# Transposes of the next group's tokens as steps among the current group's slices

## The chip, the cores and the metric

The kernel runs on one core of one Trainium2 chip. The metric is the time of one execution in microseconds on the device (us). TensorE is called PE here (its weight loads PEld), VectorE DVE, ScalarE ACT, GpSimd POOL, and SyncE, which issues all transfers of this kernel, SP.

## The reference

Three layers follow each other: causal attention blended with a linear memory, then two gated feed-forward layers over all tokens (4 batches of 576 tokens, 8 heads of 64, 512 channels, 1536 hidden channels).

```python
scores = where(causal, -1e9, q @ k.T / sqrt(D));  a = softmax(scores)
local = a @ v
q_p = phi(q)                                    # elu + 1
mem = (q_p @ M_prev) / (q_p @ z_prev + 1e-6)
x = g * mem + (1 - g) * local                   # g = sigmoid(beta), by head
x = x / sqrt(mean(x * x) + 1e-6) * rms_g
x = (silu(x @ w_gate) * (x @ w_val)) @ w_out    # layer 0
x = (sigmoid(x @ w_gate2) * (x @ w_val2)) @ w_out2   # layer 1
```

## The kernel before, in words

The tokens are worked in five groups. Group -1 holds the first 128 tokens of each of the four batches (512 tokens); its attention is done before everything else (`att_first`). Groups 0 to 3 are the other 448 tokens of batches 0 to 3. The outer loop `for g in range(-1, B)` runs the two feed-forward layers of group g, and among their work it does the attention of group g+1. Group 3 has no attention beside it.

A layer has 12 slices of 128 hidden channels. `hidden` makes a slice's gate `pg` and value `pv` (12 matmuls each, L502; two PSUM buffers of the pool `psm` for both), ACT and DVE make the product `t` from them (L517, L519 and L520 in layer 0, L517 and L522 in layer 1) and split it into two parts `h` (L524 on ACT, L525 on DVE), and `out_share` adds the slice's share into four PSUM tiles `po` (L536, L539). After the last slice `evacuate` empties the four `po`: into the next layer's input `x` (L545 on ACT, L546 on DVE), or to the output (L557, L559). In group -1 the weights come from 64-bit floats (L453, L456) and are split in two parts (L427, L428), in group 0 they are split once more and the parts stored, later groups load the parts. PE works most products three times, high by high, high by low and low by high.

Attention comes as a list of 30 steps for a group (`att_steps`): one that loads the values `v` into the tile `x` and scales them (`att_v`: the loads L125 and L126, then the maximum `am` over the tile on DVE, L128), for each head `att_qk` and `att_scores` (matmuls L186 into tiles of the PSUM pool `psa`, which has two buffers of tag `pa`; DVE and ACT work L264 to L306, L177 to L180), `att_av` (L313 to L324), for each pair of heads `att_mem` (L357 to L386), and at the end `att_norm`. `x` has one buffer: the values of group g+2 can be loaded only when the tokens of group g+1 have been read out of it.

After 23 of the 24 slices of a group, and after all its steps, `run_xT` turned the next group's tokens: four times `att_xT`, which normalises 128 tokens (`xn`, L403 on DVE), transposes them with four matmuls (`pxt`, L408, a tile of the same two `pa` buffers), and copies them out in two parts (L412 on ACT, L413 on DVE) into `xt`, the input of the next group's layer 0.

Steps are taken by the count of slices whose share has been added, `done`:

```python
while used < len(steps) and used < len(steps) * done // total:
    steps[used]()
    used += 1
```

with `total` = 21. This gives the order in which the program is written. The build then schedules the instructions by a timeline of its own (`schedule_with_timeline_sim=True`), so each engine's final order can differ from it; it is fixed before the run, and each engine works through its own list in order.

Of the kernel before, what the change touches and what calls it, by code (L numbers as in the profile page):

```python
# [33 lines left out]
def attn_moe_moe_kernel(ctx, tc, qT, kT, v, mz, beta, w8, rms_g, outT):  # L34
# [11 lines left out]
    NF = w8.shape[1]  # L46
# [66 lines left out]
    for i in range(2):  # L113
        t = const.tile([128, S], F32R, name=f"q2_{i}")
# [6 lines left out]
    st = {}  # L121
# [266 lines left out]
    def att_norm(g, t0, t1):  # L388
        x = st[g]["x"]
        ss = ap_.tile([128, 4], F32, tag="ss", bufs=2, name="ss")  # L390
        for t in range(t0, t1):
            junk = z["s", t, 0] if g < 0 else ap_.tile([128, DM], F32, tag="xn", bufs=2, name="junk")
            nc.scalar.activation(out=junk, in_=x[:, t, :], func=AF.Square, accum_out=ss[:, t:t + 1])
        s_ = ss[:, t0:t1]
        nc.vector.tensor_scalar(out=s_, in0=s_, scalar1=1.0 / DM, scalar2=1e-6, op0=ALU.mult, op1=ALU.add)
        if t0 == 0:
            st[g]["ri"] = ap_.tile([128, 4], F32, tag="ri", name="ri")
        nc.gpsimd.tensor_tensor(out=st[g]["ri"][:, t0:t1], in0=s_, in1=half_neg[:, t0:t1], op=ALU.pow)

    def att_xT(g, t, xt):  # L400
        s = st[g]
        xn = z["s", t, 1] if g < 0 else ap_.tile([128, DM], F32, tag="xn", bufs=2, name="xn")
        nc.vector.scalar_tensor_tensor(  # L403
            out=xn, in0=s["x"][:, t, :], scalar=s["ri"][:, t:t + 1], in1=g_bc, op0=ALU.mult, op1=ALU.mult
        )
        ps = psa.tile([128, KD, 128], F32, tag="pa", name="pxt")
        for k in range(KD):
            nc.tensor.transpose(ps[:, k, :], xn[:, k * 128:(k + 1) * 128], ident)  # L408
        o = 64 if g >= 0 and t == 3 else 0
        c0 = 128 * t  # L410
        n = 128 - o
        nc.scalar.copy(out=xt[:, 0, :, c0:c0 + n], in_=ps[:, :, o:128])  # L412
        nc.vector.tensor_tensor(  # L413
            out=xt[:, 1, :, c0:c0 + n],
            in0=ps[:, :, o:128],
            in1=xt[:, 0, :, c0:c0 + n].bitcast(F32),
            op=ALU.subtract,
        )
# [20 lines left out]
    for i in range(2):  # L439
        t = const.tile([128, 512], I32, name=f"top{i}")  # L440
# [128 lines left out]
    def xtile(name):  # L569
        return xp.tile([128, 2, KD, NMAX], F32R, tag=name, name=name)  # L570

    def att_steps(g):
        yield lambda: att_v(g)

        for h in range(H + 1):
            if h < H:
                yield lambda h=h: att_qk(g, h)
                yield lambda h=h: att_scores(g, h)
            if h > 0:
                yield lambda h=h: att_av(g, h - 1)  # L580
                if h % 2 == 0:
                    yield lambda h=h: att_mem(g, h // 2 - 1)
        yield lambda: att_norm(g, 0, 4)

    def att_first():
        att_load0()
# [12 lines left out]
                att_xT(-1, b - 1, xt)  # L599
        return xt  # L600

    def run_xT(g):
        xt = xtile("xt")
        for t in range(4):
            att_xT(g, t, xt)
        return xt

    xt = att_first()
    zctx.close()
# [5 lines left out]
    for g in range(-1, B):  # L615
        n = 512 if g < 0 else S - 128
        steps = list(att_steps(g + 1)) if g + 1 < B else []
        total = 2 * NF - 3
        done, used = 0, 0
        nxt = None  # L620
        for l in range(2):

            early = 2 if g < 0 and l == 0 else 0
            ws = [weights(g, l, f) for f in range(early)]
            hs = [htiles(g) for f in range(early)]
            for o, m in ((0, 256), (256, 256)):
                for f in range(early):
                    hidden(ws[f], l, f, m, g, xt, hs[f], o)
            po = None
            for f in range(NF + 1):  # L630
                if f < NF:
                    if f >= early:
                        ws.append(weights(g, l, f))
                        hs.append(htiles(g))
                        hidden(ws[f], l, f, n, g, xt, hs[f])
                    if g < 0 and l == 0 and f == 2:
                        gated.close()
                if f > 0:
                    if po is None:
                        po = [pso.tile([128, NMAX], F32, tag=f"po{d}", name="po") for d in range(KD)]  # L640
                    out_share(ws[f - 1], hs[f - 1], po, f - 1, n)
                    done += 1
                    while used < len(steps) and used < len(steps) * done // total:
                        steps[used]()
                        used += 1
                    if l == 1 and f == NF - 1 and steps:
                        nxt = run_xT(g + 1)
            xn = xtile("x1") if l == 0 else None
            for d in range(KD):
                evacuate(l, d, n, g, po[d], xn)  # L650
            xt = xn
        xt = nxt


# [42 lines left out]
```

## Time and profile before

| | |
|---|---|
| time, median of 3 runs | 1137.54 us (1136.85 to 1138.85) |
| the profiled execution's time | 1135.08 us |
| its span, first to last instruction | 1132.9 us |
| busy in the span: PE, PEld | 1094.8 us, 939.1 us |
| busy in the span: DVE, ACT, POOL | 698.5 us, 486.5 us, 74.3 us |
| mean granted clock of PE | 0.983 |

2.2 us of the profiled execution lie around its span. Busy times are sums over a span in which the stages differ much: by the slices of the page DVE is 5 to 8 tenths busy up to group 2 and 1 to 2 tenths in group 3. The busy time of PE counts each matmul to its modelled end, which overlaps the start of the next.

### The profile page before, as it was taken

How to read it: one execution, taken by the hardware profiler on the slowest of the kernel's cores; microseconds unless marked ns; L12 is line 12 of the kernel's file. 1: busy time of each engine (PE TensorE's matmuls, PEld its weight loads, DVE VectorE, ACT ScalarE, POOL GpSimd, SP SyncE). 2: the span in 40 equal slices, each digit the busy share in tenths (PEclk: the TensorE clock that was granted, in tenths of full speed). 3: DMA queues.
4: the chain of work that ended last, by engine and by line, in shares of the span. 5: the costliest groups of instructions: out<-in, count | busy, mean ns of one | idle time of the engine just before them, and what ended most of it. 6: DMA issues, size and time to landing. Idle time of an engine off the chain costs nothing.

```text
span 1132.9 us, 17438 instructions
## 1 busy us (share of the span) xinstructions
PE 1094.8 (97%) x6388; PEld 939.1 (83%) x6388; DVE 698.5 (62%) x1470; ACT 486.5 (43%) x904; POOL 74.3 (7%) x63
## 2 busy tenths in 40 slices
PE   8789999999999999998999999989999999999998
PEld 5666667666589999997999999879999998998997
DVE  6796678675688888866847655575666544222111
ACT  5775556564455556543424433342343323112111
POOL 1210000000000000000100001000010000000000
PEclk8899999999989999998999999999999999999999
DMA  6788788686869989976766667666666557766661
GB/s 183 226 299 298 253 257 273 203 265 215 297 213 331 320 298 309 315 255 227 220 215 216 212 212 217 221 212 217 212 209 205 193 176 223 216 210 210 215 213 62
DMA packets 99524, 264.07 MB, mean 233 GB/s; under 512 B 13296, under 2 KB 23536, under 8 KB 99440
## 3 DMA queue, kind: packets, MB, share of 16 engines
q1 hardware_dynamic: 99440, 262.97, 71.2%
q8 instruction: 51, 0.84, 0.3%
q14 instruction: 33, 0.27, 0.1%
HBM read 201.58 MB, written 61.34 MB: 232 GB/s over the span
## 4 chain that ended last, share of the span: by engine, by line
PE 87%; DMA 5%; DVE 4%; ACT 2%; issue 1%; SPq 1%; POOL 0%; DVEq 0%; ACTq 0%
PE pg L502 25%; PE pv L502 25%; PE po L539 20%; PE po L536 6%; PE ps L186 4%; DMA raw<-in_w 2%; PE pm L371 2%; DMA x<-in_v 1%; PE pav L313 1%; PE pav L315 1%; PE pav L314 1%; DMA q<-in_qT 1%; SPq L200 1%; DVE am L128 0%; ACT top L453 0%
## 5 line engine op out<-in xcount | busy, mean ns | idle before, releaser
L539 PE MATMUL po<-h,wl 128*128 128x448 f32 x768 | 170.4, 367 | 0.0
L517 ACT ACTIVATE t<-pg 128x448 f32<-128x448 f32 (+2 forms) x122 | 66.4, 545 | 207.6 <-PE pg L502 207.6
L539 PEld LDWEIGHTS po<-h,wl 128*128 128x128 f32 x768 | 143.4, 188 | 12.4
L502 PE MATMUL pg<-xt,wl 128*128 128x448 f32 (+1 forms) x468 | 113.6, 393 | 9.1 <-DVE t L519 6.1
L502 PE MATMUL pg<-x,wl 128*128 128x448 f32 (+1 forms) x480 | 114.5, 378 | 0.7 <-ACT t L517 0.7
L502 PE MATMUL pv<-xt,wl 128*128 128x448 f32 (+2 forms) x492 | 110.1, 368 | 0.0
L502 PE MATMUL pv<-x,wl 128*128 128x448 f32 (+1 forms) x468 | 109.9, 373 | 0.0
L502 PEld LDWEIGHTS pg<-xt,wl 128*128 128x128 f32 x468 | 91.8, 200 | 21.6 <-DVE t L519 7.3
L524 ACT CAST h<-t 128x448 fp32r<-128x448 f32 x96 | 54.2, 564 | 120.1 <-DVE t L522 60.1
L297 POOL PARTITION_ALL_REDUCE mb<-mx x32 | 55.5, 1735 | 679.0 <-DVE mx L293 601.2
L502 PEld LDWEIGHTS pv<-xt,wl 128*128 128x128 f32 x492 | 90.8, 189 | 9.6
L502 PEld LDWEIGHTS pg<-x,wl 128*128 128x128 f32 x480 | 88.5, 188 | 12.3 <-ACT t L517 1.9
L522 DVE SCALAR_TENSOR_TENSOR t<-t,pv 128x448 f32<-128x448 f32 (+1 forms) x60 | 37.9, 632 | 93.0 <-PE pv L502 81.9
L502 PEld LDWEIGHTS pv<-x,wl 128*128 128x128 f32 x468 | 87.2, 188 | 9.4
L536 PE MATMUL po<-t,wo 128*128 128x512 f32 x192 | 86.2, 592 | 0.0
L539 PE MATMUL po<-h,ws 128*128 128x448 f32 x384 | 85.4, 369 | 0.1
L453 ACT ACTIVATE top<-raw 128x512 f16<-128x512 bf16 x72 | 56.4, 785 | 56.0 <-DMA raw<-in_w 42.3
L525 DVE TENSOR_TENSOR h<-t,h 128x448 fp32r<-128x448 f32 x96 | 59.8, 622 | 30.5 <-ACT h L524 30.2
L269 ACT COPY sc<-ps 128x448 f32<-128x448 f32 (+3 forms) x128 | 47.6, 374 | 71.1 <-DVE sc L264 45.8
L539 PEld LDWEIGHTS po<-h,ws 128*128 128x128 f32 x384 | 71.6, 188 | 6.7 <-DVE h L525 0.2
L519 DVE SCALAR_TENSOR_TENSOR t<-t,pg 128x448 f32<-128x448 f32 (+2 forms) x62 | 38.2, 616 | 57.6 <-ACT t L517 57.4
L536 PEld LDWEIGHTS po<-t,wo 128*128 128x128 f32 x192 | 36.2, 189 | 36.8 <-issue 34.7
(133 smaller groups left out, 1924.6 us busy)
## 6 DMA issues: line engine op xcount, KB each, us to landing
wl<-parts SPq DMA_DIRECT2D x144, 512.0 KB, 4.1
ws<-parts SPq DMA_DIRECT2D x72, 512.0 KB, 3.9
raw<-in_w SPq DMA_DIRECT2D x72, 511.8 KB, 5.1
parts<-wl SPq DMA_DIRECT2D x48, 512.0 KB, 4.1
w<-kept SPq DMA_DIRECT2D x72, 256.0 KB, 4.6
kept<-w SPq DMA_DIRECT2D x48, 256.0 KB, 3.9
parts<-ws SPq DMA_DIRECT2D x24, 512.0 KB, 4.3
kd<-in_kT SPq DMA_DIRECT2D x64, 144.0 KB, 4.3
```

Of the source, the lines that this page charges most:

```text
L186: nc.tensor.matmul(ps[:, c0:c0 + n], kk[:, k0:k0 + 128], r[:, q0:q0 + n], start=(i == 0), stop=(i == 1 and not mask))
L269: nc.scalar.copy(out=sc[:, d:d + n], in_=ps[:, c:c + n])
L297: nc.gpsimd.partition_all_reduce(mb[:, 0:448], mx[:, 0:448], channels=128, reduce_op=bass_isa.ReduceOp.max)
L453: nc.scalar.activation(out=top.bitcast(F16).rearrange("p (n t) -> p n t", t=2)[:, :, 1], in_=raw.bitcast(BF16)[:, :, 2], func=AF.Copy)
L502: nc.tensor.matmul(ps[:, 0:n], w[:, a, k * 128:(k + 1) * 128], x[:, b, k, o:o + n], start=(i == 0), stop=(i == 3 * KD - 1))
L517: nc.scalar.activation(out=t, in_=pg[:, 0:n], func=AF.Tanh, scale=0.5)
L519: nc.vector.scalar_tensor_tensor(out=t, in0=t, scalar=1.0, in1=pg[:, 0:n], op0=ALU.add, op1=ALU.mult)
L522: nc.vector.scalar_tensor_tensor(out=t, in0=t, scalar=1.0, in1=pv[:, 0:n], op0=ALU.add, op1=ALU.mult)
L524: nc.scalar.copy(out=hh[:, 0, 0:n], in_=t)
L525: nc.vector.tensor_tensor(out=hh[:, 1, 0:n], in0=t, in1=hh[:, 0, 0:n].bitcast(F32), op=ALU.subtract)
L536: nc.tensor.matmul(po[d][:, 0:n], w[2][:, c], t[:, 0:n], start=(f == 0), stop=(f == NF - 1))
L539: nc.tensor.matmul(po[d][:, 0:n], w[2][:, a, c], hh[:, b, 0:n], start=(f == 0 and i == 0), stop=(f == NF - 1 and i == 2))
```

## The change

The four calls of `att_xT` become steps 31 to 34 at the end of `att_steps`; `next_xT` takes a new tile `xt` at the first of them and keeps it in `st`. `run_xT` after slice 23 is gone. `total` is 20, so the list of 34 steps is to be used up when 20 of the 24 slices have been added: by the formula 34*done//20, `att_norm` comes at slice 18 (it came at 21), two transposes at slice 19 and two at slice 20 (all four came at 23), and 20 instead of 17 steps lie in the 12 slices of layer 0.

```diff
@@ att_steps
         yield lambda: att_norm(g, 0, 4)
+        for t in range(4):
+            yield lambda t=t: next_xT(g, t)
@@
-    def run_xT(g):
-        xt = xtile("xt")
-        for t in range(4):
-            att_xT(g, t, xt)
-        return xt
+    def next_xT(g, t):
+        if t == 0:
+            st["xt"] = xtile("xt")
+        att_xT(g, t, st["xt"])
@@ for g in range(-1, B):
-        total = 2 * NF - 3
+        total = 2 * NF - 4
         done, used = 0, 0
-        nxt = None
@@
                         steps[used]()
                         used += 1
-                    if l == 1 and f == NF - 1 and steps:
-                        nxt = run_xT(g + 1)
@@
-        xt = nxt
+        xt = st.pop("xt", None)
```

PE where group 1 ends and group 2 begins, before (the names: `x_6808` is layer 1's input in group 1, `xt` the turned tokens of group 2, `ps` the scores of group 3's first head):

```order
L502 MATMUL pv<-x_6808,ws 128x448 x11
L539 MATMUL po<-h,wl 128x448 x12
L539 MATMUL po<-h,ws 128x448 x12
L408 MATMUL pxt<-ident,xn 128x128 x16
L502 MATMUL pg<-xt,wl 128x448
L502 MATMUL pv<-xt,wl 128x448
L186 MATMUL ps_8114<-qq,kk 128x448
L186 MATMUL ps_8114<-q_0_125,kk 128x448
L502 MATMUL pg<-xt,wl 128x448 x11
L502 MATMUL pv<-xt,wl 128x448 x11
```

The same place with the change (`x_6906` is layer 1's input in group 1):

```order
L502 MATMUL pv<-x_6906,wl 128x448 x11
L408 MATMUL pxt<-ident,xn 128x128 x8
L502 MATMUL pv<-x_6906,wl 128x448
L539 MATMUL po<-h,ws 128x448 x12
L502 MATMUL pg<-x_6906,wl 128x448 x12
L502 MATMUL pv<-x_6906,wl 128x448 x6
L408 MATMUL pxt<-ident,xn 128x128 x8
L502 MATMUL pv<-x_6906,wl 128x448 x6
L539 MATMUL po<-h,wl 128x448 x12
L502 MATMUL pg<-x_6906,ws 128x448 x12
L186 MATMUL ps_8063<-qq,kk 128x448
L186 MATMUL ps_8063<-q_0_125,kk 128x448
```

All 16 transposes stood behind the last share of group 1 and directly ahead of group 2's first matmul. Now they stand in two batches with 31 matmuls between them, and behind the second batch follow 48 more matmuls of group 1 and the first scores; group 2's first `pg` comes after these.

DVE at the same place, before:

```order
L403 SCALAR_TENSOR_TENSOR xn<-x,ri,g_bc 128x512 x2
L557 TENSOR_SCALAR o<-po 128x448
L403 SCALAR_TENSOR_TENSOR xn<-x,ri,g_bc 128x512 x2
L413 TENSOR_TENSOR xt<-pxt,xt 128x4x128 x2
L557 TENSOR_SCALAR o<-po 128x448
L413 TENSOR_TENSOR xt<-pxt,xt 128x4x128
L359 TENSOR_SCALAR phe<-phe 128x448
L413 TENSOR_TENSOR xt<-pxt,xt 128x4x64
L360 SCALAR_TENSOR_TENSOR ph<-ph,phe 128x448
L128 TENSOR_REDUCE am<-x 128x1
L519 SCALAR_TENSOR_TENSOR t<-t,pg 128x448
```

and with the change (L522 and L525 belong to slices of group 1's layer 1):

```order
L403 SCALAR_TENSOR_TENSOR xn<-x,ri,g_bc 128x512 x4
L522 SCALAR_TENSOR_TENSOR t<-t,pv 128x448
L413 TENSOR_TENSOR xt<-pxt,xt 128x4x128 x2
L525 TENSOR_TENSOR h<-t,h 128x448
L128 TENSOR_REDUCE am<-x 128x1
L413 TENSOR_TENSOR xt<-pxt,xt 128x4x128
L359 TENSOR_SCALAR phe<-phe 128x448
L413 TENSOR_TENSOR xt<-pxt,xt 128x4x64
L522 SCALAR_TENSOR_TENSOR t<-t,pv 128x448
L135 TENSOR_SCALAR ex<-amx 128x1
```

`am`, which reads the values that are loaded into `x` for group 3, stood directly ahead of the first `t` of group 2's layer 0. Now it stands two slices of group 1 earlier, ahead of the last two copies of `xt` and of a slice's L522.

DVE at the change of layers in group 1, before (`sc`, `mb`, `pt` are the softmax of a head, `mt` and `x` the sums of memory and local attention):

```order
L324 TENSOR_TENSOR x<-pav,r_6616 128x4x64
L519 SCALAR_TENSOR_TENSOR t<-t,pg 128x448
L520 TENSOR_TENSOR t<-t,pv 128x448
L180 TENSOR_TENSOR pt<-sc,pt 128x1536
L525 TENSOR_TENSOR h<-t,h 128x448
L264 TENSOR_TENSOR sc<-ps_6689,tri 128x128
```

and with the change, from the third row behind the same L519 on:

```order
L339 TENSOR_SCALAR r_6729<-pm 128x4
L323 TENSOR_TENSOR r_6714<-r_6714,ga 128x4
L340 RECIPROCAL r_6729<-r_6729 128x4
L324 TENSOR_TENSOR x<-pav,r_6714 128x4x64
L341 TENSOR_TENSOR r_6729<-r_6729,gate 128x4
L342 TENSOR_TENSOR mt<-pm,r_6729 128x256
L298 TENSOR_TENSOR sc<-sc,mb 128x896
L306 TENSOR_TENSOR sc<-sc,mb 128x320
L306 TENSOR_TENSOR sc<-sc,mb 128x192
L306 TENSOR_TENSOR sc<-sc,mb 128x128
L386 TENSOR_TENSOR x<-x,mt 128x2x128
L520 TENSOR_TENSOR t<-t,pv 128x448
```

In the last slice of layer 0, L520 followed L519 directly. Now attention's work on three tiles stands between the two.

## Rows read from the trace of the kernel before

**Rows 1.** The page: span, and busy time of each engine.

```profile
span 1132.9 us, 17438 instructions
PE 1094.8 (97%) x6388; PEld 939.1 (83%) x6388; DVE 698.5 (62%) x1470; ACT 486.5 (43%) x904; POOL 74.3 (7%) x63
```

**Rows 2.** PE in order of time, group -1 to 0: start, us, what, [idle before].

```profile
309.18 1.04 PE L408 MATMUL pxt<-ident,xn 128*128 128x128 f32 x8
312.58 1.34 PE L408 MATMUL pxt<-ident,xn 128*128 128x128 f32 x8 [2.37 <-DVE xt L413]
314.62 0.74 PE L502 MATMUL pg<-xt,wl 128*128 128x448 f32 x1 [0.69 <-ACT xt L412]
...
316.28 4.27 PE L502 MATMUL pg<-xt,wl 128*128 128x448 f32 x11
320.39 2.38 PE L502 MATMUL pv<-xt,wl 128*128 128x448 f32 x11
```

**Rows 3.** The same, group 0 to 1.

```profile
521.17 1.03 PE L408 MATMUL pxt<-ident,xn 128*128 128x128 f32 x8
523.97 1.23 PE L408 MATMUL pxt<-ident,xn 128*128 128x128 f32 x8 [1.76 <-DVE xt L413]
...
527.67 4.31 PE L502 MATMUL pg<-xt,wl 128*128 128x448 f32 x11
...
535.91 2.67 PE L502 MATMUL pg<-xt,wl 128*128 128x448 f32 x12 [0.74 <-DVE t L519]
538.42 0.25 PE L186 MATMUL ps<-qq,kk 128*128 128x192 f32 x1
```

**Rows 4.** The same, group 1 to 2.

```profile
733.36 1.03 PE L408 MATMUL pxt<-ident,xn 128*128 128x128 f32 x8
...
747.57 4.02 PE L502 MATMUL pg<-xt,wl 128*128 128x448 f32 x12 [2.97 <-DVE t L519]
751.42 0.25 PE L186 MATMUL ps<-qq,kk 128*128 128x192 f32 x1
```

**Rows 5.** The same, group 2 to 3.

```profile
943.83 1.03 PE L408 MATMUL pxt<-ident,xn 128*128 128x128 f32 x8
...
947.18 1.04 PE L408 MATMUL pxt<-ident,xn 128*128 128x128 f32 x8
...
949.51 2.48 PE L502 MATMUL pg<-xt,wl 128*128 128x448 f32 x11
```

**Rows 6.** Stretches: us, busy time of each engine, granted clock (PEclk), DMA.

```profile
521.00:538.00 17.00, 13.68 (x60) 11.87 (x59) 10.67 (x21) 5.45 (x12) 0.38 (x1) 0.80 0.71 240
943.00:957.00 14.00, 13.37 (x72) 11.91 (x71) 7.17 (x12) 4.52 (x9) 0.00 (x0) 1.00 0.72 228
```

**Rows 7.** The chain of work at group 0 to 1: start, us, what.

```profile
518.88 2.46 PE po L539 x12
521.33 0.45 PE pxt L408 x4
...
524.25 8.16 DMA x<-in_v
...
532.51 2.82 DVE am L128
```

**Rows 8.** DVE's instructions by line: busy us, mean ns, idle before.

```profile
L298 DVE TENSOR_TENSOR sc<-sc,mb 128x896 f32<-128x896 f32 x32 | 34.6, 1082 | 0.2 <-POOL mb L297 0.2
L306 DVE TENSOR_TENSOR sc<-sc,mb 128x320 f32<-128x320 f32 (+2 forms) x96 | 30.7, 374 | 0.0
L386 DVE TENSOR_TENSOR x<-x,mt 128x256 f32<-128x256 f32 x32 | 13.5, 423 | 0.6
```

**Rows 9.** Layer 0 of groups 0 and 1; columns as in rows 6.

```profile
314.00:417.00 103.00, 102.30 (x608) 93.89 (x609) 86.74 (x173) 57.52 (x101) 7.04 (x5) 0.97 0.87 299
526.00:629.00 103.00, 102.25 (x606) 93.67 (x607) 66.95 (x138) 39.08 (x65) 7.61 (x5) 0.97 0.68 218
```

## Prediction

> **What bounds the kernel now.** The profile's page first: PE is busy for 1094.8 of 1132.9 us [rows 1], no other engine comes near, so the time is PE's list of instructions and the pauses in it. What can be won is a pause or a slow stretch of PE; what can be lost is a new pause. The next view is therefore PE in order of time at the four places where one group ends and the next begins, since there the transposes stood.
>
> At the first of them PE makes eight transposes, stands idle for 2.37 us until DVE's L413 has emptied a tile, makes eight more, and waits again for `xt` (0.69 us) [rows 2]. Behind that, eleven matmuls of 448 columns take from 316.28 to 320.39, 0.37 us each [rows 2], where twelve took 2.46 us before the place, 0.205 us each [rows 7]: these run at half the clock. The stretches say the same: over 521 to 538 the granted clock was 0.80 on average (1.0 is 2.4 GHz, the lower level is 1.2 GHz), over 943 to 957 it was 1.00 [rows 6], and there PE stood still hardly at all [rows 5].
>
> The second and third place have one pause more, ahead of the next slice (0.74 and 2.97 us, for DVE's L519) [rows 3, 4]. The chain of work shows what is behind it: `am` waits on DVE for the load of `v`, which took 8.16 us, then works 2.82 us, and L519 stands behind it [rows 7]. The load cannot go out before the transposes' L403 has read `x`.
>
> **What is lost at the four places.** For each, the time from the first transpose to a point where PE is back at full clock, less what the same instructions take without pauses: 0.112 us for a transpose [rows 7], 0.205 us for 448 columns [rows 7], scores (`ps`) by their columns.
>
> - Group -1 to 0: 309.18 to 320.39 is 11.2 us [rows 2]. 16 transposes (1.8), 13 matmuls of `pg` and `pv` (2.7) and two scores (0.4) make 4.9. Lost: 6.3.
> - Group 0 to 1: 521.17 to 538.42 is 17.25 us [rows 3]. 16 transposes (1.8), 36 matmuls (7.4), eight scores of 2816 columns together (1.3) make 10.5. Lost: 6.8.
> - Group 1 to 2: the same instructions, 733.36 to 751.42, 18.05 us [rows 4]. Lost: 7.6.
> - Group 2 to 3: eight transposes and two matmuls from 947.18 to 949.51 take 2.3 us for 1.3 of work [rows 5]; the first batch already lay among matmuls. Lost: 1.0. There is no group 4 whose `v` would be loaded.
>
> Together 21.7 us. The work itself stays: every transpose, normalisation, copy and load is still issued, as often as before.
>
> **What the change gives back.** In the order with the change the batches of transposes stand 31 matmuls apart (6.4 us at 0.205), so the emptying of the first two tiles, which cost 2.37 us in the open [rows 2], is covered; 48 matmuls and two scores follow the second batch (10 us) before group 2's first `pg` reads `xt`. `evacuate` of the old group now stands beside the new group's first two slices: the first new share into `po` comes some 27 matmuls (5.5 us) after the last old one, for four copies on two engines. I cost both at nothing; if that cover failed, it would be the old pauses again, 2 to 3 us a place. The clock then has no reason to fall: at group 2 to 3 one batch stood among matmuls, and it did not [rows 5, 6].
>
> What could move along is the wait of the second batch itself: it waited for L413 because `pa` has two buffers, 2.37 and 1.76 us at the first two places [rows 2, 3], and with the third taken like the second 5.9 us of the 21.7 would stay. By the rows the wait is for a copy that takes little over 2 us, and the order now has 6.4 us of work ahead of it, so I keep none of it in the sum. The Trainium skill holds a rule on this against the change: "Perfetto Trace Analysis", section "Optimization Strategy", says that a gap which repeats on the engine that should be full can mean too few SBUF or PSUM buffers for the next tile, and by it moving the work would not help. The trace so far agrees that the gap is one of buffers, and not that it must follow the transposes.
>
> **What it adds: three things.**
>
> First, `am` now stands inside group 1 (and 0, and -1), ahead of two copies of `xt` and of a slice's L522. At group 1 to 2, counted from the end of the first batch: before, at group 0 to 1, the load landed at 532.4, 10.3 us after that batch (521.17 and eight transposes) [rows 3, 7]; half a microsecond of this was an output's issue that stood between the two loads of `v` and no longer does (an estimate), which leaves 9.8; `am` takes 2.8 [rows 7], the next L413 some 0.7: 13.3 us. PE has by then one `pv`, `po`, `pg`, `pv`, a batch, `po` and `pg` to do, 61 matmuls and eight transposes, 13.4 us; next come scores that need this L413's buffer, and a `pv` that needs that L522. It is a tie: between nothing and 2 us; I take 0.5. At group 0 to 1 `am` stands behind the copies, at -1 to 0 slices are longer (512 columns, and `po` from 32-bit tiles): nothing for either. The lower end is 0, since the load cannot make PE faster than full; the upper end, 2 us at each of three places, 6.
>
> Second, at the changes of layer, L520 of the last slice stands behind attention's work on DVE: L298 1.08, three L306 of 0.37, L342, L386 and L324 of 0.42 each [rows 8], with small rows some 4 us. PE has attention's short products and twelve `pv` (2.5 us and more) until L520 could start at all, then a `po` (2.46) before it needs L525. I take 0.3 us for each of groups 0, 1 and 2; the bounds are 0 and 2 each.
>
> Third, attention is denser: 34 steps in 20 slices against 30 in 21, so 1.7 a slice against 1.43, and 20 steps instead of 17 in layer 0. DVE was busiest in layer 0 of group 0, 86.7 of 103 us, and PE was busy for 102.3 of them [rows 9]. In group 1, where no weights are split, DVE's whole work in this layer was 67 us [rows 9]; even if all of that were attention, 3 steps in 17 more would add 11.8: 98.5 of 103, and PE's share of the three steps lengthens the layer too. It does not saturate on average, but single slices can. I take 2 us in the whole run for it; the bounds are 0 and 8 (a quarter of a microsecond for each of 32 heads).
>
> Sum: 21.7 - 0.5 - 0.9 - 2 = 18.3 us. The profiled execution, 1135.1 us (1132.9 span), would become 1116.8. The median of the three runs was 1137.5, 2.4 above it; on that footing **1119 us**.
>
> **The rivals.**
>
> 1. *Part of the pauses comes back at the new places* (the two `pa` buffers, slices whose DVE work is late, a fall of the clock behind one of them: the pause of 0.74 us came while the clock was already low [rows 3, 6], and one of 2.97 was followed by twelve matmuls in 3.85 us instead of 2.46 [rows 4]). For it: DVE at 84% in one layer [rows 9]. Against: PE was busy through 102.3 of 103 us beside it [rows 9]. With 5.9 for the buffers, or with 3 us and one slow stretch at two of the seven places, 6 to 11 us more than my sum: 1125 to 1130.
> 2. *The load of `v` holds DVE at three places.* If it takes 3 us longer there than the 8.2 measured, since more weight loads run beside it, PE stands 3 us and falls to the low clock each time (about 1.4 us as in rows 4): 13 us, 1132.
> 3. *Slower: DVE becomes the bound in groups -1 and 0.* If the denser steps make PE wait in each head's softmax, the time goes above the old one from 0.7 us a head on (21.7 over 32 heads). At 0.8 us for each, 1141. Against it stand the 16 us that DVE had free in its fullest layer [rows 9], with at most 12 to be added.
> 4. *No change*: the places stay as they are because `am`, not the transposes, ends the wait there. But `am` ends only the last pause of the second and third place [rows 3, 4], and it moves as well. 1137.
>
> **How the numbers follow.** My forecast (gain 15 to 24) has 0.58, rival 1 has 0.27, rival 2 0.08, rival 3 0.04, no change 0.03. The forecast's own range is 1114 to 1122: the whole 21.7 plus 2 us as the best, the costs at 7 us as the worst. For 8 in 10 I go from 1113 over rival 1's upper end to 1130. A measurement of this kernel can tell about 0.2% (2.3 us) from no change. Faster by over that: the forecast and rivals 1 and 2, 0.93; within: 0.03; slower: 0.04.
>
> **What would show it.** In the new trace PE should have no pause over 1 us at the group changes, granted clock 1.00 through them, and next-group `pg` directly behind old `pv` and `po`. L128 should still wait for the load, 5 us or more on DVE, with PE working meanwhile. L413's third copy should follow `am` at the change of group 1 to 2. PE's pauses at the changes of layer should stay under 1 us. I am wrong if PE waits for DVE's L520, L522 or L306 in the middle of groups -1 and 0, or if the clock shows low stretches at places that had none.

## The result and the profile after

The changed kernel took 1111.7 us (median of 4 runs, 1110.8 to 1112.6), the kernel before on the same chip 1137.5 (4 runs, 1136.9 to 1138.9): a ratio of 0.977, interval 0.976 to 0.979, a gain of 25.8 us. The forecast was 1119, from 1113. The profiled execution took 1112.6 us against 1135.1, 22.5 less. Repeated on two other chips the ratio was 0.984 (0.981 to 0.988) and 0.981 (0.979 to 0.983), gains of 18.6 and 22.2 us by the medians; why it differs is part of what follows.

The page after, which answers to [rows 1]:

```profile
span 1110.7 us, 17453 instructions
PE 1084.4 (98%) x6388; PEld 933.4 (84%) x6388; DVE 694.8 (63%) x1470; ACT 486.0 (44%) x904; POOL 76.7 (7%) x63
```

Each engine has as many instructions as before, so the span shrank by 22.2 us of pauses and slow matmuls. The stretches around the four group changes, and layer 0 of group 1 (columns as in [rows 6]):

```profile
300.00:320.00 20.00, 20.00 (x81) 14.68 (x80) 13.00 (x28) 9.28 (x17) 0.00 (x0) 1.00 0.84 298
505.00:525.00 20.00, 20.00 (x103) 18.54 (x102) 14.21 (x30) 9.09 (x18) 0.63 (x1) 1.00 0.72 239
712.00:735.00 23.00, 23.00 (x116) 20.80 (x115) 17.42 (x39) 10.05 (x20) 0.39 (x2) 1.00 0.72 238
915.00:935.00 20.00, 20.00 (x99) 18.24 (x98) 5.27 (x10) 4.42 (x8) 0.00 (x0) 1.00 0.73 236
...
515.00:618.00 103.00, 103.00 (x669) 95.00 (x668) 66.82 (x147) 39.94 (x65) 8.71 (x5) 1.00 0.70 227
```

PE is busy through all four changes, at full clock; in [rows 6] it stood still for 3.3 of 17 us and had 0.80. DVE's work in the first 103 us of group 1, again from its first `pg` on, is 66.8 us, as it was [rows 9]: the steps that came into this layer are matched by the work on `v` that left it.

PE in order of time at group 0 to 1, which answers to [rows 3]:

```profile
500.87 1.03 PE L408 MATMUL pxt<-ident,xn 128*128 128x128 f32 x8
...
515.39 2.61 PE L502 MATMUL pg<-xt,wl 128*128 128x448 f32 x12
517.83 0.36 PE L502 MATMUL pv<-xt,wl 128*128 128x448 f32 x1
518.03 0.98 PE L539 MATMUL po<-h,ws 128*128 128x448 f32 x4
518.85 0.37 PE L502 MATMUL pv<-xt,wl 128*128 128x448 f32 x1
519.06 1.80 PE L539 MATMUL po<-h,ws 128*128 128x448 f32 x8
520.70 2.23 PE L502 MATMUL pv<-xt,wl 128*128 128x448 f32 x10
```

The new group's `pg` is finished before the old group's last share into `po`; no row carries an idle time, and twelve matmuls take 2.6 us where eleven took 4.3 [rows 3].

**Where the time went.** For every matmul of a trace I took the time from its start to the next one's start, less the median of its line and shape in the trace of before. Summed by place this is PE's lost time in us (the group changes from 3 us ahead of the first transpose to 30 us behind it; "start" is all up to 92 us, "layer, group -1" 180 to 212 us):

| profile | span | start | group changes, each | together | layer, group -1 | elsewhere |
|---|---|---|---|---|---|---|
| before | 1132.9 | 28.5 | 6.2, 6.6, 7.5, 0.9 | 21.1 | 0.5 | 4.5 |
| after | 1110.7 | 28.6 | -0.1, -0.3, 0.0, -0.2 | -0.6 | 3.5 | 0.9 |

The 22.2 us are 21.7 at the group changes and 3.6 elsewhere, less 3.0 that are new at one change of layer.

What is new there stands at the change of layer in group -1: two pauses, which cost 0.8 and 1.8 us of these 3.0. PE, then DVE, then ACT, in order of time, after:

```profile
188.03 0.97 PE L502 MATMUL pg<-x,wl 128*128 128x512 f32 x3 [0.65 <-DVE x L546]
197.93 2.37 PE L502 MATMUL pg<-x,wl 128*128 128x512 f32 x9 [1.67 <-ACT t L517]
```

```profile
185.31 1.76 DVE L180 TENSOR_TENSOR pt<-sc,pt 128x1536 f16<-128x1536 f32 x1 [1.91 <-ACT pt L179]
...
187.29 0.68 DVE L546 SCALAR_TENSOR_TENSOR x<-po,x 128x512 fp32r<-128x512 f32 x1
```

```profile
196.66 0.78 ACT L453 ACTIVATE top<-raw 128x512 f16<-128x512 bf16 x1 [1.47 <-DMA raw<-in_w]
197.31 0.57 ACT L517 ACTIVATE t<-pg 128x512 f32<-128x512 f32 x1
```

The first pause is DVE's: attention's L180 stands ahead of L546, which makes layer 1's input. The second is ACT's: a conversion of weights stands at the head of its queue and waits for its transfer; the slice's L517, for which PE waits, stands behind it. Of the 3.6 us that went elsewhere, 2.2 were one place of this second kind in the kernel before, also in group -1, again PE and then ACT:

```profile
283.98 3.07 PE L502 MATMUL pg<-x,wl 128*128 128x512 f32 x12 [0.39 <-ACT t L517]
289.56 0.20 PE L315 MATMUL pav<-vh,pt 128*128 128x65 f16 x1 [1.03 <-DVE pt L180]
```

```profile
282.82 0.63 ACT L427 ACTIVATE wl<-w 128x512 fp32r<-128x512 f32 x1 [4.99 <-DMA w<-kept]
```

There L427 waited for its weights ahead of an L517, and the late work behind it on ACT and DVE made the second pause. From that change of layer to the end of group -1 the changed kernel loses 0.7 us, where 3.1 were lost.

### The profile page after: what moved, and what is told of

Same layout as the page of the kernel before. It is cut to its first block, busy times and chain, and to the rows that moved or that the text cites. A ratio compares the mean times of both kernels' runs of the same rounds, so it can differ in the third digit from the quotient of the medians.

```text
span 1110.7 us, 17453 instructions
## 1 busy us (share of the span) xinstructions
PE 1084.4 (98%) x6388; PEld 933.4 (84%) x6388; DVE 694.8 (63%) x1470; ACT 486.0 (44%) x904; POOL 76.7 (7%) x63
## 4 chain that ended last, share of the span: by engine, by line
PE 92%; DMA 4%; DVE 1%; SPq 1%; ACT 1%; issue 0%; POOL 0%; DVEq 0%; ACTq 0%
PE pg L502 27%; PE pv L502 26%; PE po L539 21%; PE po L536 6%; PE ps L186 4%; DMA raw<-in_w 2%; PE pm L371 2%; PE pav L313 1%; PE pav L315 1%; PE pav L314 1%; DMA kept<-w 1%; PE pxt L408 1%; DMA kept<-wo 1%; DMA q<-in_qT 1%; SPq L200 1%
## 5 line engine op out<-in xcount | busy, mean ns | idle before, releaser
L517 ACT ACTIVATE t<-pg 128x448 f32<-128x448 f32 (+2 forms) x122 | 66.6, 546 | 202.4 <-PE pg L502 202.3
L502 PE MATMUL pg<-xt,wl 128*128 128x448 f32 (+1 forms) x468 | 107.3, 377 | 2.4 <-DVE t L519 2.4
L502 PEld LDWEIGHTS pg<-xt,wl 128*128 128x128 f32 x468 | 87.2, 190 | 12.8 <-DVE t L519 3.2
L522 DVE SCALAR_TENSOR_TENSOR t<-t,pv 128x448 f32<-128x448 f32 (+1 forms) x60 | 37.9, 631 | 93.2 <-PE pv L502 89.5
L525 DVE TENSOR_TENSOR h<-t,h 128x448 fp32r<-128x448 f32 x96 | 60.3, 628 | 29.2 <-ACT h L524 28.8
L519 DVE SCALAR_TENSOR_TENSOR t<-t,pg 128x448 f32<-128x448 f32 (+2 forms) x62 | 38.2, 616 | 59.3 <-ACT t L517 58.8
L427 ACT ACTIVATE wl<-w 128x512 fp32r<-128x512 f32 x78 | 49.0, 630 | 48.5 <-PE po L539 15.4
L269 ACT COPY sc<-ps 128x448 f32<-128x448 f32 (+3 forms) x128 | 47.5, 375 | 47.3 <-DVE sc L264 26.5
```

The costliest lines, as they stand in the source:

```text
L269: nc.scalar.copy(out=sc[:, d:d + n], in_=ps[:, c:c + n])
L427: nc.scalar.activation(out=w[:, 0], in_=raw, func=AF.Copy)
L502: nc.tensor.matmul(ps[:, 0:n], w[:, a, k * 128:(k + 1) * 128], x[:, b, k, o:o + n], start=(i == 0), stop=(i == 3 * KD - 1))
L517: nc.scalar.activation(out=t, in_=pg[:, 0:n], func=AF.Tanh, scale=0.5)
L519: nc.vector.scalar_tensor_tensor(out=t, in0=t, scalar=1.0, in1=pg[:, 0:n], op0=ALU.add, op1=ALU.mult)
L525: nc.vector.tensor_tensor(out=hh[:, 1, 0:n], in0=t, in1=hh[:, 0, 0:n].bitcast(F32), op=ALU.subtract)
```

## The experiments

My theory was that the gain is the loss at the group changes, and that it takes two things: attention must end early enough for the tokens to be read out of `x`, and the transposes and the load of `v` must come early enough for the load (some 8 us) and `am` (2.8) to lie under the old group's matmuls. The rivals are named with each run. Where several kernels are compared in words, they ran on one chip, and the kernel before beside them; its median was 1134.5 us for the first four runs, 1134.5 for the second four, and 1135.9 for the third.

### The two parts of the change, one at a time

The pace alone: before with `total` of the change, transposes still behind slice 23.

```diff
-        total = 2 * NF - 3
+        total = 2 * NF - 4
```

> The kernel before with one edit: its 30 steps are due by slice 20 instead of 21; the transposes stay behind slice 23. Theory (the gain is the pauses and slow stretches at the four group changes, and density alone gives nothing): those places keep their 21.7 us, the time stays at 1137 within 3 us (ratio 0.997 to 1.003). Rival (the 4 us by which the spans differ more than I forecast come from attention ending earlier, which leaves DVE and ACT free in the last slices of group -1): 1133 to 1134, and the pause of 2 us that the kernel before has near 283 to 290 us is gone.

1127.4 us, ratio 0.994 (0.991 to 0.996): faster than either had said. The group changes lose 9.5 us instead of 21.1; 4.0 are lost anew at the change of layer in group -1. The reason is in the built order: since attention ends a slice earlier, the build spread part of the transposes by itself (eight, a share of `po`, eight), though they are written last. Another 3 us are lost at the change of layer of group 0, at the new pace. What the build could not move is the load. PE and DVE at group 0 to 1:

```profile
524.17 2.38 PE L502 MATMUL pg<-xt,wl 128*128 128x448 f32 x11
...
532.47 4.13 PE L502 MATMUL pg<-xt,wl 128*128 128x448 f32 x12 [2.83 <-DVE t L519]
```

```profile
529.07 2.82 DVE L128 TENSOR_REDUCE am<-x 128x1 f32<-128x2560 f32 x1 [4.72 <-DMA x<-in_v]
531.81 0.61 DVE L519 SCALAR_TENSOR_TENSOR t<-t,pg 128x448 f32<-128x448 f32 x1
```

`am` still stands directly ahead of the new group's L519, and the pause is still followed by a stretch at half the clock. A pace still denser does not help:

```diff
-        total = 2 * NF - 3
+        total = 2 * NF - 6
```

> The kernel before with only its count of slices changed, from 21 to 18: attention of the next group ends three slices earlier, the transposes are still written after slice 23. Theory (both levers are needed: an earlier end lets the values' load go out early only if the tokens have been read out of x early, and that is done by the transposes' normalisation, which the program order still puts last): the group changes keep 5 us and more, and the denser attention costs something besides; 1124 to 1130. Rival (the pace alone is enough, since the scheduler moves the normalisation and the transposes up once attention has ended): 1111 to 1116.

1128.7 us, ratio 0.995 (0.993 to 0.997). As the theory said: 8.2 us stay at the group changes, and PE now pauses at the changes of layer of groups 1 and 2 as well (1.64 and 1.92 us for ACT's L269), 3.9 us more elsewhere than before.

The steps with a slower pace: the changed kernel with all of them due by slice 23, where attention ends at slice 21 as in the kernel before, and by slice 21 (`- 3` for `- 1` in this diff), where it ends at 19.

```diff
-        total = 2 * NF - 4
+        total = 2 * NF - 1
```

> The changed kernel with its 34 steps due by slice 23 instead of 20. In the built order the transposes lie among matmuls, as in the changed kernel, but the reduction am (L128) stands directly ahead of the next group's first L519 again, as in the kernel before, and the load of v can go out only some two slices later than in the changed kernel. Theory (two causes at the group changes, the transposes' own pauses and the wait for v): the pauses for L413 and L412 (8.3 us) and their slow clock go, a wait for L128 of 3 to 6 us stays at group changes 0 to 1 and 1 to 2, now the only one there, with a fall of the clock behind it: 1120 to 1127. Rival (the wait for v only showed because PE had been held up before it; due times don't matter as long as the transposes lie among matmuls): 1111 to 1114.

> The changed kernel with its 34 steps due by slice 21 instead of 20. Theory (any due time that leaves the load of v some 13 us of PE's work does): no pause at the group changes, and 1110 to 1113. Rival (slice 20 is needed, one slice later the wait for v is back): 1115 to 1120.

Due by 23: 1126.1 us, ratio 0.992 (0.989 to 0.995), as the theory said. Due by 21: 1115.7 to 1115.9 in three runs and 1127.2 in a fourth at a lower clock (0.977 against 0.990), ratio with all four 0.987 (0.981 to 0.992): the rival's number, since one slice later the wait is back. With 23 the group changes lose 12.3 us, with no idle time ahead of a transpose; with 21 they lose 3.6 at group 0 to 1 and nothing at the others. DVE and PE at group 0 to 1, due by 23:

```profile
523.63 2.82 DVE L128 TENSOR_REDUCE am<-x 128x1 f32<-128x2560 f32 x1 [3.12 <-DMA x<-in_v]
526.37 0.61 DVE L525 TENSOR_TENSOR h<-t,h 128x448 fp32r<-128x448 f32 x1
```

```profile
527.04 3.34 PE L539 MATMUL po<-h,ws 128*128 128x448 f32 x8 [2.31 <-DVE h L525]
```

and PE due by 21:

```profile
518.15 1.91 PE L539 MATMUL po<-h,ws 128*128 128x448 f32 x8 [1.23 <-DVE h L525]
...
527.35 0.47 PE L186 MATMUL ps<-qq,kk 128*128 128x448 f32 x1 [2.17 <-DVE sc L264]
```

The first pause is `am` each time, now ahead of L525 of the old group's last slices. The second of the kernel due by 21 is the work on `v` that follows `am`; DVE there:

```profile
525.49 1.40 DVE L150 SCALAR_TENSOR_TENSOR vl<-x,sv,vh 128x512 f16<-128x512 f32 x2
526.81 0.48 DVE L264 TENSOR_TENSOR sc<-ps,tri 128x128 f32<-128x128 f32 x2
```

So the pauses are not a matter of where the transposes stand by themselves; they go as far as the load, `am` and what follows on `v` get away from the end of the group. The pace alone gives 7 us, the steps at the old pace 8, the two together 18.6 to 25.8.

### Does the clock fall for the pauses, or by itself?

The kernel before with sixteen short matmuls of no use (their result is overwritten) ahead of the first `pg` of groups 0 to 3, to keep PE at work there:

```diff
@@
+NFILL = 16
@@ hidden
+        if g >= 0 and l == 0 and f == 0:
+            for i in range(NFILL):
+                nc.tensor.matmul(pg[:, 0:384], tri_b, ident_b[:, None, :].to_broadcast([128, 3, 128]), start=True, stop=True)
```

> The kernel before with 16 useless matmuls of 384 columns (bfloat16) put in front of the first real matmul of each of groups 0 to 3, into the same PSUM tile, which the real ones overwrite. They add 64 x 0.16 = 10 us of work, some of it in the pauses. Theory (about a third of the loss at the group changes, 6.8 us, is the slow clock behind a pause, and goes when PE does anything in the pause): granted clock 1.00 through the first two changes, matmuls of 0.205 us behind them, the pause for L128 still there at the third; time 1131 to 1137. Rival (the clock falls whatever stands in the pause): matmuls of 0.37 us stay, and the useless work adds up: 1140 to 1147.

1140.2 us, ratio 1.005 (1.003 to 1.006). At group -1 to 0, where three fillers and four matmuls of the old group came to lie in the wait for L413, eleven `pg` went at full clock (2.38 us, against 4.27 in [rows 2]). At group 0 to 1 the build put `am` ahead of a copy of `xt` and PE stood for 5.89 us; the next eleven took 4.31 (PE in order of time, line numbers shifted by one):

```profile
533.30 0.74 PE L187 MATMUL ps<-qq,kk 128*128 128x448 f32 x1 [5.89 <-DVE xt L414]
534.21 4.31 PE L503 MATMUL pg<-xt,wl 128*128 128x448 f32 x11
```

The clock is as the theory said, full where PE was kept busy, and the time is the rival's. The 64 fillers took 11.2 us themselves, and the group changes still lost 17.2: PE's waits behind `am` came to 9.6 us at three places (2.02, 5.89 and 1.69), where they were 3.7 at two [rows 3, 4]. The order changed along, so this run does not weigh one pause alone.

### Four steps or one

```diff
-        for t in range(4):
-            yield lambda t=t: next_xT(g, t)
+        yield lambda: [next_xT(g, t) for t in range(4)]
```

> The changed kernel with the four transposes as one step instead of four: 31 steps are spread instead of 34, all four transposes fall due together at slice 20. In the built order they stand as eight and eight with a slice's share between them, am behind the first batch or behind both. Theory (what counts is that they are written by slice 20; that they are separate steps counts for nothing): no pause over 1 us at the group changes, 1110 to 1113. Rival (the spacing over two slices is what hides the emptying of their two tiles): 2 us a place are back, 1116 to 1119.

1124.6 us, ratio 0.991 (0.989 to 0.994): neither had it. The emptying of the tiles was not the trouble: no idle time stands ahead of a transpose. But the first batch of group 0 to 1 came 14.3 us later than in the change (508.5 against 494.2), and DVE's `am` stood ahead of an L525 (DVE, then PE):

```profile
518.56 2.82 DVE L128 TENSOR_REDUCE am<-x 128x1 f32<-128x2560 f32 x1 [3.05 <-DMA x<-in_v]
521.30 0.62 DVE L525 TENSOR_TENSOR h<-t,h 128x448 fp32r<-128x448 f32 x1
```

```profile
521.97 3.35 PE L539 MATMUL po<-h,ws 128*128 128x448 f32 x8 [2.99 <-DVE h L525]
```

That place lost 6.6 us, and the change of layer of group 0 another 3.1. Four steps count one by one in the list and so pull all others forward; with one, the formula (30 of 31 steps, by slice 20) gives `att_norm` slice 20 instead of 18.

### The edge at group 1 to 2

The changed kernel again, on two other chips, first with these expectations:

> The changed kernel again, beside the others of its chip. Theory (the gain is the pauses and low-clock stretches at the group changes, which the kernel before has in numbers that differ from run to run, 2.4 to 6 us of spread, and the changed kernel lacks): 1110 to 1113 us, runs within 2 us of each other, ratio to the kernel before 0.976 to 0.980 by medians. Rival (1111.7 was a lucky set of runs, and the profiled rows of before with their 18.3 were right): 1115 to 1119, with a spread like the kernel before's.

> The changed kernel a third time, beside the two below. Theory (its runs differ because at group 1 to 2 the load of v and am end at the very time at which PE needs the copy L413 behind them; a load that lands 2 us later becomes a pause of 1.6 us, and some of these pauses bring a low-clock stretch): 1111 to 1121 us, median 1112 to 1116, and the runs with the lowest granted clock the longest ones. Rival (the longer runs of the first repetition were one disturbed chip): all runs within 1110 to 1113.

1115.9 us (1112.9 to 1120.8) and 1113.7 (1111.7 to 1116.0), where the first chip had given 1111.7. The theory's 1110 to 1113 of the first repetition failed, and its rival's number came, for another reason; the second came as its theory said, the longest run at the lowest clock (0.985 against 0.992 for the shortest). In the trace of the first repetition DVE, and then PE, at group 1 to 2:

```profile
710.80 2.82 DVE L128 TENSOR_REDUCE am<-x 128x1 f32<-128x2560 f32 x1 [8.10 <-DMA x<-in_v]
713.54 0.68 DVE L413 TENSOR_TENSOR xt<-pxt,xt 128x512 fp32r<-128x512 f32 x1
```

```profile
714.27 0.47 PE L186 MATMUL ps<-qq,kk 128*128 128x448 f32 x1 [1.57 <-DVE xt L413]
```

In the trace of the first chip the load landed 1.9 us sooner, and PE did not pause:

```profile
710.43 2.82 DVE L128 TENSOR_REDUCE am<-x 128x1 f32<-128x2560 f32 x1 [6.17 <-DMA x<-in_v]
713.17 0.68 DVE L413 TENSOR_TENSOR xt<-pxt,xt 128x512 fp32r<-128x512 f32 x1
```

To test it, the maximum of group 3's values was taken over the tile twice in one instruction, which lengthens `am` at this place alone and leaves the order up to the pause as it was (behind it the build put two scores after the `pv`, and more shifted with them):

```diff
-            out=am, in_=x.rearrange("p t d -> p (t d)"), op=ALU.max, axis=AX.X, apply_absolute_value=True
+            out=am, in_=(x.rearrange("p t d -> p (t d)").unsqueeze(1).to_broadcast([128, 2, 5 * DM]) if g == 3 else x.rearrange("p t d -> p (t d)")), op=ALU.max, axis=(AX.XY if g == 3 else AX.X), apply_absolute_value=True
```

> The changed kernel with the maximum am of group 3's values taken twice over in one instruction, so that it takes 5.6 us instead of 2.8 at the change of group 1 to 2 and nowhere else; the order of the instructions is the same. Theory (am, and with it L413, has next to no cover there): PE pauses 2.4 to 4.8 us for L413 there, and the time is 2.4 to 8 us above that of the changed kernel on this chip, the upper part with a low-clock stretch behind the pause. Rival (am is covered by several us and the spread comes from other places): under 1 us.

1118.6 us against 1113.7 for the changed kernel beside it. DVE and PE:

```profile
715.54 5.49 DVE L128 TENSOR_REDUCE am<-x 128x1 f32<-128x5120 f32 x1 [7.56 <-DMA x<-in_v]
720.95 0.68 DVE L413 TENSOR_TENSOR xt<-pxt,xt 128x512 fp32r<-128x512 f32 x1
```

```profile
721.68 0.74 PE L186 MATMUL ps<-qq,kk 128*128 128x448 f32 x1 [3.70 <-DVE xt L413]
722.22 0.57 PE L186 MATMUL ps<-q,kk 128*128 128x448 f32 x1
722.60 4.68 PE L502 MATMUL pv<-x,ws 128*128 128x448 f32 x12
```

`am` is 2.67 us longer, and PE pauses 3.70, with the next twelve matmuls at half the clock. Since the order differs behind the pause, it is the pause that this run weighs, and not all of the 4.9 us. The profiles with this order at group 1 to 2 (two of them are told below):

| | after | repeated on the third chip | slice 21 in group -1 | single run | repeated on the second | lengthened |
|---|---|---|---|---|---|---|
| DVE's wait ahead of `am`, us | 6.17 | 7.00 | 7.40 | 7.54 | 8.10 | 7.56 + 2.67 |
| PE's idle time for L413, us | 0 | 0.47 | 0.87 | 1.01 | 1.57 | 3.70 |

Wherever there is a pause, it is the wait less 6.53 us. In two more profiles with this order the wait was shorter, 5.92 and 5.97 us, and PE did not pause. The old group's matmuls cover 6.53 us of DVE's wait, and the load leaves between nothing and 1.6 above it.

### Other due slices

Due slice 21 in group -1 alone, twice, and together with 19 in groups 0 to 2 (`else 5` in this diff):

```diff
-        total = 2 * NF - 4
+        total = 2 * NF - (3 if g < 0 else 4)
```

> The changed kernel with due slice 21 in group -1 and 20 in groups 0 to 2. Theory (the pauses of 0.7 and 1.7 us at the change of layer in group -1 come from the pace there, which puts more of attention and of the late weight transfer into one stretch of ACT's queue): they go, and the first group change stays clean, 1108 to 1110. Rival (the pauses come from the transfer of the weights alone, whatever the pace): 1111 to 1112; and if the wait behind am returns at the first group change, as it did at one place with due slice 21 everywhere, 1113 to 1115.

> Due slice 21 in group -1 and 20 in groups 0 to 2, a second time, to tell it from the changed kernel on one chip. Theory (it saves the pauses of about 2 us at the change of layer in group -1 and keeps the edge at group 1 to 2): 1.5 to 3 us under the changed kernel's median here, with the same spread. Rival (the 4.7 us between the two in the batch before were the luck of four runs): the same as the changed kernel within 1 us.

> The changed kernel with due slice 21 in group -1, 20 by default replaced by 19 in groups 0 to 2. In the built order am at group 1 to 2 then stands behind all four copies of xt, as it already does at group 0 to 1; at group 0 to 1 it now stands between them. Theory (the edge moves to group 0 to 1, where the load starts a slice earlier than before): 1109 to 1113 us, spread under 4 us, no pause over 1 us at group 1 to 2. Rival (the denser attention of groups 0 to 2 makes PE wait in single slices or at the changes of layer): 1113 to 1117, the pauses in the middle of these groups.

The first gave 1111.1 us (1110.1 to 1113.9) beside 1115.9 for the changed kernel, its repetition 1115.7 (1112.1 to 1116.9) beside 1113.7: no difference that holds, the second above both its numbers, and 1.5 and 2.6 us were still lost at the change of layer in group -1. But they were lost at another instruction. PE's wait for L517, behind ACT's late weights, had gone (nothing in the first, 0.18 us in the second); its wait for L546 had grown from 0.65 us to 0.88 and 1.25. PE, then DVE, in the first:

```profile
188.47 0.95 PE L502 MATMUL pg<-x,wl 128*128 128x512 f32 x3 [0.88 <-DVE x L546]
```

```profile
186.26 0.95 DVE L306 TENSOR_TENSOR sc<-sc,mb 128x320 f32<-128x320 f32 x3
...
187.73 0.68 DVE L546 SCALAR_TENSOR_TENSOR x<-po,x 128x512 fp32r<-128x512 f32 x1
```

So each side was half right: the pause for ACT's weights went, as the theory said, and much of the loss stayed, as the rival said, but because attention's L306 and a conversion of weights (L456) now stood ahead of L546.

Slices 21 and 19 together gave 1112.5 us (1110.4 to 1115.3) beside 1113.7: by the time alone not to be told from the change, with a spread of 4.8 us where under 4 was expected, but its trace shows the edge gone. DVE at group 1 to 2:

```profile
698.10 0.69 DVE L413 TENSOR_TENSOR xt<-pxt,xt 128x512 fp32r<-128x512 f32 x1 [2.86 <-ACT xt L412]
699.00 0.42 DVE L413 TENSOR_TENSOR xt<-pxt,xt 128x256 fp32r<-128x256 f32 x1
699.62 2.82 DVE L128 TENSOR_REDUCE am<-x 128x1 f32<-128x2560 f32 x1 [0.20 <-DMA x<-in_v]
```

`am` waits 0.20 us and stands behind all copies.

### What differs from run to run

One profiled run each, two of the kernel before and two of the changed one, on one chip:

> The kernel before once more, one profiled run. Theory (the footing differs because the first 85 us hold more or less time at the low clock in either kernel, whatever the change): if its granted clock over the first 85 us is 0.90, as in the two profiles first compared, 1134 to 1136 us; if it is 0.80 to 0.84, 2.5 to 4.5 us more by that alone. About 20 us lost at the group changes, and the two pauses of 1 to 1.3 us near 283 and 288 us in group -1. Rival (the 2.4 us between its profiled run and its median lie at the group changes): 24 us and more lost there, the first 85 us as before.

> The same as the run before this one; the two together show how much the losses at the group changes and in the first 85 us differ between two runs of one kernel. Theory: the group changes differ by under 3 us, the first 85 us by up to 4.5. Rival: the other way round.

> The changed kernel, one more profiled run. Theory: PE's pause at group 1 to 2 is what DVE waits for the load of v ahead of am, less 6.2 us, and nothing below that (0 at 6.2, 0.8 at 7.0, 1.9 at 8.1 us in the three profiles so far); the time is 1111 us with a granted clock of 0.90 in the first 85 us and up to 1115 with 0.80, plus this pause. Rival (the longer runs lose their time in the middle of the groups): the pause as said, the first 85 us at 0.90, and the time above 1113 all the same.

> The same as the run before this one. Theory: the difference of the two times is that of their first 85 us and of their pause at group 1 to 2, within 1 us. Rival: over 2 us of it lie elsewhere.

They took 1131.1, 1142.1, 1122.7 and 1120.7 us. PE's lost time, as in the table above:

| profile | span | start | group changes, each | together | layer, group -1 | elsewhere |
|---|---|---|---|---|---|---|
| before, first | 1128.9 | 27.2 | 6.2, 5.8, 6.5, 0.9 | 19.4 | 0.5 | 3.4 |
| before, second | 1140.0 | 31.0 | 6.3, 10.4, 9.1, 0.9 | 26.7 | 0.4 | 3.6 |
| changed, first | 1120.8 | 38.7 | -0.1, -0.3, 1.4, -0.2 | 0.8 | 1.9 | 1.1 |
| changed, second | 1118.8 | 38.0 | -0.1, -0.3, -0.2, -0.2 | -0.8 | 2.3 | 1.1 |

For the kernel before both sides were half right, and its first run was shorter than the theory's 1134. The 11 us between its two runs are 7.3 at the group changes, which the theory had put under 3, and 3.8 at the start. At the second change of its longer run the load of `v` took 9.55 us instead of 7.34, PE waited for L519, and the clock fell:

```profile
538.98 4.85 PE L502 MATMUL pg<-xt,wl 128*128 128x448 f32 x12 [3.56 <-DVE t L519]
```

At the third change the load took as long in either run (7.94 and 7.89 us), and the clock made the difference. The same pauses for L413 and L412 (1.77 and 0.81 us) were followed by eleven matmuls in 4.31 us in the first run and in 2.38 in the second; PE then waited 0.52 us for L519 in the first, and 3.22 with a fall of the clock behind it in the second.

For the changed kernel the places are as the theory said: the two runs differ by 2.0 us, of which 0.7 lie at the start and 1.6 in the pause at group 1 to 2, and that pause was 7.54 - 6.53 = 1.01 us in the one and nothing in the other. (The expectation's 6.2 counts lost time, 0.37 more than the idle time of the rows.) What makes both long is the start: 10 us more than in the table of after, where 4 had been allowed. The stretch from 12 to 46 us and the first 85 us, after, then the first of these two:

```profile
12.00:46.00 34.00, 29.14 (x214) 26.11 (x215) 29.05 (x107) 26.03 (x94) 6.46 (x9) 0.90 0.65 190
0.00:85.00 85.00, 66.86 (x389) 52.29 (x390) 66.86 (x181) 56.26 (x155) 17.00 (x26) 0.90 0.75 236
```

```profile
12.00:46.00 34.00, 32.55 (x142) 29.13 (x143) 20.52 (x72) 19.70 (x78) 3.94 (x5) 0.50 0.38 98
0.00:85.00 85.00, 71.62 (x360) 58.45 (x360) 57.33 (x165) 49.74 (x146) 16.19 (x25) 0.74 0.67 214
```

The clock was at its lower level, 1.2 GHz, for those 34 us, in a part of the program that the change does not touch.

## Why the prediction was right or wrong

**The loss at the four places, 21.7 us.** Right in mechanism and size: 21.1 became -0.6 in the two profiles first compared. PE has no pause and a clock of 1.00 through all four. Both halves were needed: with the steps at the old pace no pause stood ahead of a transpose, and 12.3 us were still lost, behind `am` and the work on `v` that follows it.

**The emptying of the two `pa` buffers.** It costs nothing, as I had it; rival 1, which kept 5.9 us for it, falls. Of the rule in the Trainium skill, "Perfetto Trace Analysis", section "Optimization Strategy", that a repeating gap can mean too few buffers, nothing was left here: with the same two buffers the gap went, and the trace of the pace alone shows the batches apart without it too. The rule says only that a gap can mean this; that moving the work would then not help was my step, and it does not hold here. This is one case of moved work, and does not show that more buffers would not have done it as well. Behind the second batch at group 1 to 2 the trace has 54 matmuls and four scores (12.2 us), where I had counted 48 and two (10 us).

**First cost, `am` at group 1 to 2, 0.5 us with bounds 0 and 2.** The place and the bounds were right, and it is the one edge of the new order: 0 in the profile first compared, 0.47 to 1.57 us in other runs. At the other two places it cost nothing. The warning in rival 2, a load that takes longer by 3 us, did not come; 1.9 us did, at one place.

**Second cost, changes of layer, 0.9.** Nothing in groups 0 to 2. The pauses that came, 3.0 us more lost, were in group -1, for which I had put nothing. The first of them is this term's own mechanism, attention's work on DVE ahead of what the next layer needs, at L546 instead of L520. The second I had not looked for: ACT's queue, where a transfer of weights ends the wait.

**Third cost, denser attention, 2 us with bounds 0 and 8. This is the step that failed.** I had bounded it from below by nothing, as if a new order could only add pauses. The kernel before lost 4.5 us elsewhere, 2.2 of it at the place behind ACT's L427; the change loses 0.9. The term was a gain of 3.6. With the loss of 3.0 in group -1, the three costs that I had put at 3.4 us came to a gain of some 0.6: 22.2 by the spans where I had 18.3. Nor did DVE get fuller in group 1 [rows 9]; I had added the three steps and not taken off the work on `v` that leaves the layer. The gain is not one of density either. The loss near 283 us is nearly gone (0.2 us left) both with the pace alone and in the kernel due by 23, where attention keeps the old pace; the second loses 1.2 us elsewhere, the first 3.3, some 3 of it at one change of layer. The gain goes with a changed order; why the weights come late ahead of an L517 in one order and not in another stays open.

**The footing, 2.4 us above the profiled run.** Also wrong: the changed kernel's median lay 0.8 below its profiled run, 3.2 us of the miss of 7.3. I had taken the distance of before for a fixed amount. It is not: the kernel before differs by 7 us between runs at the very places that the change removes, and the start differs by 4 us between its runs and by 10 between those of the changed kernel. On the other chips the gain of the medians was 18.6 and 22.2, and the times, 1115.9 and 1113.7, lie within the range of 1113 to 1130 that 1111.7 missed. That 18.6 is next to my 18.3 does not confirm the terms: the run traced there, the shortest of its four (1112.9), has those of the first chip, but for the 1.57 us pause at group 1 to 2. Which of these lengthened the timed runs of before on the first chip stays open, as they have no traces.

The rivals: 2, 3 and no change did not come. Of the signs I had named, L128's wait of 5 us and more came at group 1 to 2 alone (6.17; 3.11 and 1.17 at the others).

## What to carry to other kernels

When work that ends a stage is moved, follow what is queued behind it to its last link: here the transposes held the load, the load held `am`, and `am` held DVE's queue, and the time came back only as far as that last link moved off the end of the group. Give a term for a new order both signs: the old order has pauses of its own that the next one need not keep. A cover can be measured by lengthening the covered instruction by a known amount where the order up to the pause stays; here it gave 6.53 us to 0.01. And a pause that depends on a transfer makes the kernel's time uneven, so the gain of removing it differs from run to run as the pause did.

## What the runs showed of the hardware

- The same load of `v` (1.25 MB), issued at the same place of the same order, kept DVE waiting for 5.97 to 8.10 us in five runs of the changed kernel.
- The granted clock of the first 85 us was 0.74 to 0.90 in runs of the same program (0.50 against 0.90 from 12 to 46 us), worth up to 10 us of 1112.
- Idle times of PE of 2.83, 3.56 and 3.70 us were followed by twelve matmuls in 4.1 to 4.9 us instead of 2.46; 0.47 to 1.57 us at group 1 to 2 were followed by none at the low clock in the profiles. In between it went both ways: 2.31 us in one kernel was followed by slow matmuls (eight in 3.34), 1.23 and 2.17 us in another were not, and the same 1.77 us at group 1 to 2 of the kernel before was in one run (eleven in 4.31) and was not in another (2.38).
